# An opening written out as one list of steps, with the first phases rounded by matmul

## The chip, the cores and the metric

The kernel runs on one core of one Trainium2 chip. The core has five engines that run side by side, each through its own instructions in order: TensorE (PE, matmuls; PEld are its weight loads), VectorE (DVE), ScalarE (ACT), GpSimd (POOL) and SyncE (SP). DMA transfers are issued here from SP, POOL and ACT. The metric is the device time of one execution in microseconds (us).

## The reference

The program is a block with two parts. The first convolves a sequence of 2048 tokens with 576 channels by kernels that are sums over 128 complex poles per channel; the second is a gated MLP.

```python
dt = jnp.exp(log_dt)[:, None]
A = A_re + 1j * A_im
logdA = dt * A
P = jnp.exp(logdA[:, :, None] * l[None, None, :])
K = jnp.einsum("dn,dnl,dn->dl", Cc, P, dB).real
...
y = irfft(rfft(u) * rfft(K)) + u * Dskip
...
h = _layernorm(x) * (1 + ca) + sa
x = x + ga * _A_ref(h, ...)
h = _layernorm(x) * (1 + cb) + sb
x = x + gb * _B_ref(h, ...)
```

`sa`, `ca`, `ga`, `sb`, `cb`, `gb` are six rows of `silu(c) @ w_mod`, the modulation rows.

## The kernel before

**Poles.** `poles` turns the inputs (`A_re`, `A_im`, `log_dt` and so on) into four numbers per pole: decay, phase per step, phase per 64 steps, and the weight's logarithm and phase. Each is split in three bf16 parts (`split3`, tiles `pt`) and stored in DRAM (`pa_d` phases, `pb_d` decays), one transfer for each half of the partitions. It runs twice: for chunk 0 on tiles of 128x144, then for chunks 1 to 3 together on 128x432 (`p1`, in steps between other work). `poles_load` fetches a chunk's tables back as `lb`, `lc`, `la`.

**Groups.** 36 groups of 16 channels follow, nine per chunk. For a group g, `e_unit` builds exponents by matmul with a table of small numbers (`sel`) and takes their Exp (tile `et`); `t_unit` builds phases by matmul. For g under 10 they are rounded in PSUM: adding and taking off a large constant (`magics`) by matmul leaves the fraction; DVE copies the result to SBUF (`ft`, L479) and takes its absolute value (L484). For later groups ACT adds the constant (L482) and DVE subtracts (L483). `s_unit` takes the sine of both on ACT, of the absolute value with a quarter turn as its bias, which is the cosine (L489, L490). `p_unit` multiplies exponents with sines and cosines on DVE (L500 to L503), `kg_unit` multiplies the results into the convolution kernel on PE (L513, evacuated as `kab`, L516), `d_unit` adds the skip term, `k1_unit` applies a first transform (L530, L537).

**LN and the input.** Four `x` tiles (`ln_x`) of four rows each are normalized. `ln_stats` takes mean and variance, for the first two tiles on ACT (L397, L400), for the others by DVE's statistics instruction. `ln_pair` scales two rows, multiplies them with small transforms (L433: pieces of 32 rows by 64 columns, four row pieces by two column pieces of the array), evacuates (L435, `st1o`) and stores to `u_d`. It needs three modulation rows (`mod_unit`: 24 matmuls with `ec`, an evacuation `mpart`, two matmuls with `ones`).

**Rounds.** A loop over `tick` (a round) runs one group: exponents for three groups in every third round, phases of group `tick`, sines of `tick - 1`, `p` of `tick - 2`, `kg` and `d` of `tick - 3`, `k1` of `tick - 4`. Rounds 0 to 7 also hold the LN pairs, 3 to 5 the last modulation rows. From round 10 the transformed input is loaded (`u_load`), transformed (`u_unit`), its halves swapped by two POOL transfers, multiplied with the transformed kernel (`z_unit`, round 12 on), transformed back (`v_unit`) and stored. Chunk 1's tables are fetched in round 7, behind the last LN pair, and first used in round 9.

**What sets the order.** A scheduler orders each engine's instructions by their dependencies and the order of the code; instructions issued through a `Pin` keep the program's order. In the opening POOL's table transfers and, up to round 0, DVE and PE are pinned. Pools set how far an engine may run ahead: `ps2` gives two PSUM buffers for phases, wide exponents, LN and modulation alike, `ps1` four for the rest; `ft` has three buffers, `et` five, `ln_x`, `st1o` and `lb` two each. Behind the 40 rounds the MLP follows.

Of the kernel before, what the change touches and what calls it, by code (L numbers as in the profile page):

```python
# [9 lines left out]
F32 = mybir.dt.float32  # L10
# [21 lines left out]
def consts():  # L32
# [64 lines left out]
    sel = np.zeros((112, 2368))  # L97
    sel[:48, :1024] = sel[64:, :1024] = half
# [7 lines left out]
    sel[:48, 1024:1280] = sel[64:, 1280:1536] = rge.reshape(48, 256)  # L106
# [57 lines left out]

def ssm(tc, I, x1_d, consts_s, dram, mod_d, mlp):
# [5 lines left out]
    with ExitStack() as ctx:  # L171
# [7 lines left out]
        pa_d = dram.tile([4, 2, 9, CW // 2], BF, name="pa_d")  # L179
        pb_d = dram.tile([4, 2, 6, CW // 2], BF, name="pb_d")  # L180
# [13 lines left out]
        sel = tb.tile([112, 2368], BF, name="sel", bufs=1)  # L194
# [4 lines left out]
        def poles(c0, c1, Q, own=None):  # L199
# [8 lines left out]
            def split3(*items):  # L208

                n = 3 // (c1 - c0)  # L210
                parts = []
                for i, (src, dst, k) in enumerate(items):
                    if not todo:
                        t_ = ep.tile([128, 3, 432], BF, name="pt")
                        todo.extend(t_[:, :, w * j:w * j + w] for j in range(n))
                    parts.append((src, dst, k, todo.pop(0), t("sq%d" % (i % 2))))
                for src, dst, k, pt, q in parts:
                    A.activation(pt[:, 0], src, AF.Copy)
                    V.tensor_tensor(q, src, pt[:, 0], op=ALU.subtract)
                    A.activation(pt[:, 1], q, AF.Copy)  # L220
                for src, dst, k, pt, q in parts:
# [11 lines left out]
            def run():  # L233
# [3 lines left out]
                A.activation(dt, ldt, AF.Exp)  # L237
                V.tensor_tensor(tau, dt, tau, op=ALU.mult)
# [13 lines left out]
                ax, ay, mx, mn, ph, lw = Cr, Ci, Br, Bi, t("ph"), t("lw")  # L252
# [9 lines left out]
                AP = mlp.tied.scalar  # L262
                AP.activation(q1, mn, AF.Square)
                AP.activation(q1, q1, AF.Ln, bias=one)
                AP.activation(ph, mn, AF.Arctan)
# [4 lines left out]
                split3((al, pb_d, 0), (tau, pa_d, 0))  # L270
# [3 lines left out]
                split3((tau64, pa_d, 3), (lw, pb_d, 3))  # L274
# [15 lines left out]
                split3((ph, pa_d, 6))  # L290
# [5 lines left out]
        def poles_load(c, Q):  # L296
            for n, d_, k in (("lb", pb_d, 0), ("lc", pa_d, 0), ("la", pa_d, 3)):
                t_ = tb.tile([112, 9, 128], BF, name=n)
                if n == "lb":
                    Q.memset(t_[32:64], 0.0)  # L300
                for h in range(2):
                    Q.dma_start(t_[64 * h:64 * h + 48], d_[c, h, k:k + 6].rearrange("q (c g n) -> (q c) g n", c=8, g=9))
                lt[n, c] = t_
# [4 lines left out]
        def halves(t, gi):  # L308
            return [t[64 * h:64 * h + 48, gi] for h in range(2)]

# [15 lines left out]
        def mod_load(k):  # L326
# [6 lines left out]
            for hh in range(2):  # L333
                S.dma_start(wmt[k][hh], I["w_mod"][:, k, hh])
# [7 lines left out]
        def mod_unit(k):  # L342
            wm = wmt.pop(k)
            mpart = ep.tile([128, D], F32, name="mpart", bufs=1)
            pm = ps2()
# [5 lines left out]
            A.activation(v3(mpart), pm[:, :, :HC], AF.Copy)  # L351
# [3 lines left out]
            src = pm[:, :, :HC]  # L355
# [4 lines left out]
            elif k == 0:  # L360
                V.tensor_tensor(v3(sga), src, v3(gar), op=ALU.mult)
                for i in range(2):
                    A.activation(gsp, sga, AF.Copy)
                    V.scalar_tensor_tensor(sga, gsp, msk[:, i:i + 1], sga, op0=ALU.mult, op1=ALU.add)
                A.activation(gsp, sga, AF.Copy)
# [7 lines left out]


        x4s = {}
        r1t = {}

        def ln_load(i):
            x4s[i] = ep.tile([128, 4, D], F32, name="ln_x")
            S.dma_start(x4s[i], I["x"][:, 4 * i:4 * i + 4])  # L380

        def r1_load(i):
            r1t[i] = ep.tile([128, 2, 2, 32], F32, name="r1t"), ep.tile([128, 2, 2, 32], BF, name="cs")
            S.dma_start(r1t[i][0], I["c_r1t"][:, 2 * i:2 * i + 2])
            S.dma_start(r1t[i][1], I["c_cs"][:, 2 * i:2 * i + 2])
# [3 lines left out]
        def ln_stats(i):  # L389
            x = x4s[i]  # L390
            nm = ep.tile([128, 4], F32, name="nm")
            r = ep.tile([128, 4], F32, name="r")
            if i < 2:
                junk = ep.tile([128, 4, HC], F32, name="st1o").rearrange("p (a b) d -> p a (b d)", a=2)
                ss = ep.tile([128, 4], F32, name="ss", bufs=1)
                for b in range(4):
                    A.activation(junk[:, 0], x[:, b], AF.Copy, accum_out=nm[:, b:b + 1])  # L397
                V.tensor_scalar(nm, nm, -1.0 / D, None, op0=ALU.mult)
                for b in range(4):
                    A.activation(junk[:, 1], x[:, b], AF.Square, bias=nm[:, b:b + 1], accum_out=ss[:, b:b + 1])  # L400
                V.tensor_scalar(ss, ss, 1.0 / D, None, op0=ALU.mult)
                rsqrt(V, ep, r, ss, 4)
            else:
                bs = ep.tile([128, 4, 2, 6], F32, name="bs")
                mv = ep.tile([128, 4, 2], F32, name="mv")
                for b in range(4):
                    for h in range(2):
                        V.bn_stats(bs[:, b, h], x[:, b, HC * h:HC * h + HC])
                    V.bn_aggr(mv[:, b], bs[:, b])
                V.tensor_scalar(nm, mv[:, :, 0], -1.0, None, op0=ALU.mult)  # L410
                rsqrt(V, ep, r, mv[:, :, 1], 4)
            lns[i] = nm, r

        def ln_rows(b):
# [5 lines left out]
            V.tensor_scalar(rt, r1t[b // 2][0][:, b % 2].rearrange("p r k -> p (r k)"), r[:, j:j + 1], None, op0=ALU.mult)  # L420
            return n, rt, r1t[b // 2][1][:, b % 2].rearrange("p r k -> p (r k)")

        def ln_pair(b):
            pair = [ln_rows(b), ln_rows(b + 1)]
            for h in range(2):
                c = slice(HC * h, HC * h + HC)
                o = ep.tile([128, 4, HC], F32, name="st1o")
                pms = [ps2(), ps2()]
                for t, (n, rt, cs) in enumerate(pair):
                    for x, y, st in ((cs, gsp, True), (rt, n, False)):  # L430
                        for g in range(4):
                            rows = slice(32 * g, 32 * g + 32)
                            T.matmul(pms[g // 2][64 * t:64 * t + 64, g % 2, :HC], x[rows], y[rows, c], start=st, stop=not st, skip_group_check=True)  # L433
                for k, pm in enumerate(pms):
                    A.activation(o[:, 2 * k:2 * k + 2], pm[:, :, :HC], AF.Copy)  # L435
# [1763 lines left out]
```

## Time and profile before

| what | value |
| --- | --- |
| median of 3 runs | 1783.53 us (1782.89 to 1787.73) |
| span of the profiled execution | 1781.6 us |
| PE, DVE, ACT, POOL busy over the span | 94%, 71%, 47%, 14% |
| bytes moved by DMA | 376.24 MB, 211 GB/s |

The execution's time around its span is not recorded by itself; the median stands 1.9 us above the span. The page draws the span in 40 slices of 44.5 us; each digit is a tenth of the slice that the engine was busy, and PEclk the TensorE clock that was granted, in tenths of full speed:

```profile
PE   3687899997899999999999999999999999999999
DVE  6874999965899998698899778688344478344432
ACT  4766998854477656445434444234232223122210
PEclk9576999998899999999999999999999999999999
DMA  9456645579689879777675886874766573556531
```

The first five digits are the opening: PE and its clock are low there, and neither DVE nor ACT is full. From the fifth slice on (178 us) PE is near full. The views used below have these forms: a table of stages gives the busy time of each engine in a stretch; a group row gives line, engine, operation, output and input tiles, shapes and count, then busy us and mean ns of one, then idle time before them and what ended it; a timeline row gives start and length in us, and in brackets the idle time before it with its releaser. L152 is the line of `Pin`, so pinned instructions are told apart by their tiles.

### The profile page before, as it was taken

Reading aid. Unit: us, or ns where it says so; the run is one execution under the profiler, and the core shown is the slowest. Engines: PE = TensorE matmul, PEld = TensorE weight load, DVE = VectorE, ACT = ScalarE, POOL = GpSimd, SP = SyncE. Lnnn points to the kernel's source line nnn. Section 1 sums busy time; section 2 is a strip of 40 time slices with the busy share of each in tenths; the row PEclk is TensorE's granted clock in tenths of the full one; section 3 lists DMA queues with packets and bytes.
Section 4 is the critical chain, followed back from the end, with each engine's and each line's share of the span. In section 5 each row is a group of like instructions: output and inputs, shape, how many; then the busy total and the mean of one; then the engine's idle time right before and its main releaser. Section 6 shows DMA issues by size and latency. Waiting matters only on the chain.

```text
span 1781.6 us, 36375 instructions
## 1 busy us (share of the span) xinstructions
PE 1671.0 (94%) x15174; PEld 1242.2 (70%) x15174; DVE 1258.9 (71%) x2259; ACT 833.9 (47%) x1118; POOL 244.8 (14%) x400
## 2 busy tenths in 40 slices
PE   3687899997899999999999999999999999999999
PEld 1243555565455545777877888888888888888887
DVE  6874999965899998698899778688344478344432
ACT  4766998854477656445434444234232223122210
POOL 3312232333122211000000000000111100111100
PEclk9576999998899999999999999999999999999999
DMA  9456645579689879777675886874766573556531
GB/s 260 133 179 184 189 124 172 172 204 297 206 260 283 246 229 267 281 245 256 233 224 164 287 302 240 267 244 125 249 219 232 195 234 98 192 195 219 192 111 41
DMA packets 183381, 376.24 MB, mean 211 GB/s; under 512 B 39360, under 2 KB 103488, under 8 KB 182448
## 3 DMA queue, kind: packets, MB, share of 16 engines
q1 hardware_dynamic: 140416, 175.23, 32.7%
q0 software_dynamic: 36896, 172.01, 29.3%
q10 hardware_dynamic: 5904, 26.67, 3.7%
q8 instruction: 119, 1.95, 0.5%
q14 instruction: 46, 0.38, 0.1%
HBM read 263.11 MB, written 101.31 MB: 205 GB/s over the span
## 4 chain that ended last, share of the span: by engine, by line
PE 57%; DVE 16%; DMA 3%; issue 3%; ACT 1%; POOL 0%; ACTq 0%; SPq 0%; DVEq 0%; POOLq 0%
PE ps L152 54%; DVE bsz L152 2%; DVE zset L152 1%; DVE n L152 1%; DVE gt L152 1%; DVE rq L152 1%; DMA zset<-set_d 1%; DVE wsp L152 1%; DMA wsst<-in_w_spT 1%; DVE wso L152 1%; DVE nt L152 1%; DVE raw L152 1%; DVE rx L152 1%; DVE bsx L152 1%; DVE z L152 1%
## 5 line engine op out<-in xcount | busy, mean ns | idle before, releaser
L152 PEld LDWEIGHTS <-zset 128*128 128x128 f16 x7182 | 702.1, 98 | 91.9 <-DVE zset L152 7.6
L152 PE MATMUL ps<-wsp,zset 128*128 128x256 f16 x6048 | 667.4, 273 | 6.9 <-DVE zset L152 5.8
L152 PE MATMUL pz<-wz,nt 128*128 128x512 f16 (+1 forms) x1120 | 223.4, 360 | 8.9 <-DVE nt L152 4.2
L152 ACT ACTIVATE z<-gt 128x1024 f16<-128x1024 f32 x56 | 59.0, 1054 | 288.6 <-DVE gt L152 288.6
L152 PEld LDWEIGHTS <-nt 128*128 128x128 f16 x1120 | 109.9, 99 | 116.3 <-DVE nt L152 5.7
L152 DVE SCALAR_TENSOR_TENSOR gt<-ps,sc,bsp 128x512 f32<-128x512 f32 x36 | 27.0, 749 | 205.0 <-PE ps L152 203.3
L1907 POOL DMA_DIRECT2D zset<-set_d x96 | 50.8, 529 | 868.5 <-PE ps L152 614.6
L152 PE MATMUL ps<-wout,z 128*128 128x288 f16 x1344 | 170.0, 286 | 0.0
L152 PEld LDWEIGHTS <-z 128*128 128x128 f16 x1344 | 131.5, 98 | 33.0
L152 PE MATMUL ps<-n2o,zset 128*128 128x256 f16 x1134 | 128.2, 273 | 0.0
L152 DVE SCALAR_TENSOR_TENSOR gt<-ps,sc,gt 128x512 f32<-128x512 f32 (+1 forms) x180 | 122.2, 696 | 7.9 <-DVE gt L152 0.5
L152 DVE TENSOR_TENSOR raw<-raw 128x512 f32<-128x512 f32 (+2 forms) x228 | 119.1, 528 | 12.3 <-DMA raw<-z_d 7.9
L152 ACT ACTIVATE zset<-raw 128x1792 f16<-128x1792 f32 x48 | 81.0, 1690 | 57.8 <-PE ps L152 23.4
L152 DVE TENSOR_TENSOR zset<-raw,zset 128x1792 f16<-128x1792 f32 x48 | 96.9, 2019 | 14.9 <-ACT zset L152 14.9
L152 DVE TENSOR_TENSOR z<-ps,z 128x512 f32<-128x512 f32 (+1 forms) x126 | 71.9, 598 | 36.8 <-ACT z L152 26.7
L152 ACT ACTIVATE wsp<-raw,sc 128x1792 f16<-128x1792 f32 x25 | 44.6, 1785 | 43.0 <-DVE raw L152 35.3
L152 ACT ACTIVATE z<-z,sc 128x1024 f32<-128x1024 f32 x21 | 24.1, 1149 | 75.6 <-DVE z L152 71.9
L152 ACT ACTIVATE z<-pz,sc 128x512 f32<-128x512 f32 (+1 forms) x96 | 52.3, 579 | 15.0 <-PE pz L152 10.9
L152 PE MATMUL ps<-n2q,wf 128*128 128x512 f16 x252 | 55.7, 379 | 0.0
L152 ACT ACTIVATE z<-z,nm,r 128x1152 f32<-128x1152 f32 x24 | 31.5, 1343 | 50.3 <-DVE nm L152 28.2
L501 DVE TENSOR_TENSOR pg<-et,ft 128x1024 f32<-128x1024 f32 x36 | 43.8, 1217 | 13.3 <-ACT ft L489 11.6
L152 PE MATMUL ps<-wout,z1b 128*128 128x288 f16 x384 | 52.6, 286 | 0.5 <-ACT z1b L152 0.5
(358 smaller groups left out, 2461.9 us busy)
## 6 DMA issues: line engine op xcount, KB each, us to landing
zset<-set_d POOLq DMA_DIRECT2D x96, 896.0 KB, 4.9
raw<-z_d SPq DMA_DIRECT2D x48, 512.0 KB, 5.7
set_d<-zset ACTq DMA_DIRECT2D x24, 896.0 KB, 6.1
z_d<-z POOLq DMA_DIRECT2D x32, 576.0 KB, 9.2
zset<-wa_d POOLq DMA_DIRECT2D x18, 896.0 KB, 4.8
raw<-in_w_spT SPq DMA_DIRECT2D x25, 512.0 KB, 4.4
set_d<-zset SPq DMA_DIRECT2D x12, 896.0 KB, 5.9
u_d<-st1o POOLq DMA_DIRECT2D x16, 576.0 KB, 4.1
```

The costliest lines, as they stand in the source:

```text
L152: return self.tc.keep_in_program_order(f(*a, **k))
L501: V.tensor_tensor(pr, pi, c3[:, :, None, :].to_broadcast([128, 16, 2, 32]), op=ALU.mult)
L1907: self.nc.gpsimd.dma_start(o, self.set_d[f, j - 1] if j else self.wa_d[f])
```

## The change

Six things change.

1. **One list.** `OPENING`, a string, replaces all up to round 13: 396 steps, each a short name with indices and each meant for one engine (`eA`/`EA` exponents by matmul / Exp, `eB`/`EB` the same for the second part, `a`/`A` sine phases / sine, `c`/`C` cosine phases / cosine, `pa`/`pb` the two halves of `p`, `k`/`K` and `n`/`N` the two kernel products and their evacuations, `h`/`H`/`u` LN products, evacuation, store, `w` statistics, `r` row updates, `q` a step of the big pole chain, `mm`, `me`, `mo`, `mf` a modulation row, `X` the fetch of chunk 1's tables, `P` the change of pools). The units are cut into such parts, and all engines are pinned while the list runs. The loop then starts at round 14 with the code of before.
2. **Phases.** For groups under 14 both phases are rounded by matmul. The cosine's quarter turn is a 49th row of the tables, of ones in `lc` and `la` and of ±0.25 in `sel`. The sine reads PSUM; DVE's copy and absolute value go.
3. **LN.** Products come in steps of two row pieces (`ln_mm(j, h, k)`), one PSUM buffer each. The statistics of tile 2 are taken on ACT, of tiles 0, 1 and 3 on DVE. The transform tables of LN (`r1t`, `cs`) come in two transfers instead of sixteen.
4. **Poles.** Both halves of a stored part go in one transfer. Chunk 0's tables are fetched from SP, `lb` ahead of the others, and the big pole inputs are issued behind them.
5. **Loads.** The first `x` tiles, the first modulation row's weights (`mod_load(0)`) and the LN tables are issued from POOL.
6. **Tables of later chunks** are fetched in step `X`, and in rounds 14 and 21 (before: 7, 13 and 21); each fetch has five memsets instead of one.

```diff
+    for c0, q in ((0, 0.25), (768, 0.25), (1536, -0.25)):
+        sel[48::64, c0:c0 + (512 if c0 == 1536 else 256)] = q
...
+OPENING = (
+    "mo 2;mm 1;ml 3;mg 2;me 1;eA 0;w 0 0;mo 1;EA 0;w 0 1;eB 0;w 0 2;w 0 3;eA 1;EB 0;eB 1;EA 1;w 0 4;eA 2;EB 1;eB 2;EA 2;mm 0;EB 2;mf 1;"
+    "q 0;r 0;a 0;me 0;q 1;mo 0;mf 0;q 2;c 0;ga 0;gb 0;q 3;ga 1;gb 1;q 4;r 1;w 1 0;r 2;ga 2;A 0;w 1 1;r 3;w 1 2;h 0 0 0;C 0;w 1 3;"
...
-                        for h in range(2):
-                            Q.dma_start(dst[c, h, k:k + 3].rearrange("q (p f) -> p q f", p=64),
-                                        pt[64 * h:64 * h + 64, :, 144 * (c - c0):144 * (c - c0) + 144])
+                        Q.dma_start(dst[c, k:k + 3].rearrange("q h (p f) -> (h p) q f", p=64),
+                                    pt[:, :, 144 * (c - c0):144 * (c - c0) + 144])
...
+        def poles_tile(c, Q):
+            for n, p in (("lb", 112), ("lc", 113), ("la", 113)):
+                lt[n, c] = tb.tile([p, 9, 128], BF, name=n)
+                Q.memset(lt[n, c][32:64], 0.0 if n == "lb" else 1.0)
+                if n != "lb":
+                    Q.memset(lt[n, c][96:113], 1.0)
...
+        def ln_mm(j, h, k):
+            c = slice(HC * h, HC * h + HC)
+            pm = lno[j, h, k] = ps2()
+            for t in range(2):
+                n, rt, cs = prs[2 * j + t]
+                for x, y, st in ((cs, gsp, True), (rt, n, False)):
+                    for g in (2 * k, 2 * k + 1):
+                        rows = slice(32 * g, 32 * g + 32)
+                        T.matmul(pm[64 * t:64 * t + 64, g % 2, :HC], x[rows], y[rows, c], start=st, stop=not st, skip_group_check=True)
...
+        def phase(g, x):
             c, gi = divmod(g, 9)
+            pa = tp[g, x] = ps2()
+            hv, rw = (halves, rows) if x else (halves1, rows1)
...
-            if g < NR:
-                magics(2112, True)
-                phases((768, 0), False, False)
-                magics(2240, False)
-                phases((1536, 1792), False, True)
-                V.tensor_copy(f, pa)
...
+            magics(2112, True)
+            phases((768, 0), False)
+            magics(2240, False)
+            phases((1536, 1792), True)
+
+        def sine(g, x):
+            if x:
+                tt[g] = tb.tile([128, 2, 2, 512], F32, name="ft", bufs=3)
+            A.activation(tt[g][:, x], tp.pop((g, x)), AF.Sin, scale=-TWO_PI)
...
+        V, A, G, T, S = mlp.tied.vector, mlp.tied.scalar, mlp.tied.gpsimd, mlp.tied.tensor, mlp.tied.sync
...
+        for step in OPENING.split(";"):
+            name, *args = step.split()
+            steps[name](*map(int, args))
+        V, A, G, T, S = nc.vector, nc.scalar, nc.gpsimd, nc.tensor, nc.sync
+        for tick in range(14, NG + 4):
```

How this moves instructions at the places on which the prediction rests, first on ACT. Before, around the first sines (`ft`); `t_q` and `t_ph` belong to the big pole chain, `st1o` are LN evacuations and, with `ss`, LN statistics:

```order
L400 ACTIVATE st1o,ss<-ln_x,nm 128x576
L152 ACTIVATE t_q_307<-t_q_307,consts_s 128x432
L400 ACTIVATE st1o,ss<-ln_x,nm 128x576
L152 ACT_TABLE_LOAD
L152 ACTIVATE t_ph<-t_n_B_im 128x432
L435 ACTIVATE st1o<-ps 128x576 x2
L489 ACT_TABLE_LOAD
L489 ACTIVATE ft<-ft,consts_s 128x1024
```

After the change, from the same chain on:

```order
L154 ACTIVATE t_q_359<-t_q_359,consts_s 128x432
L154 ACTIVATE gsp<-sga 128x576
L154 ACT_TABLE_LOAD
L154 ACTIVATE ft<-ps 128x1024 x2
L154 ACTIVATE st1o<-ps 128x576
L154 ACTIVATE t_ph<-t_n_B_im 128x432
```

Sine and cosine of group 0 now stand ahead of all LN evacuations, and the arctangent (`t_ph`) follows them under the same table. The second place is POOL at the fetch of chunk 1's tables, of before (`u_d` are LN stores, `mod_d` modulation rows):

```order
L372 DMA mod_d<-gar 16x1x36
L436 DMA u_d<-st1o 128x4x288 x6
L152 MEMSET lb 32x1152
L152 DMA lb<-pb_d 48x1152 x2
L152 DMA lc<-pa_d 48x1152 x2
```

and of the change:

```order
L154 DMA u_d<-st1o 128x4x288
L154 MEMSET lb 32x1152
L154 MEMSET lc 32x1152
L154 MEMSET lc 17x1152
L154 MEMSET la 32x1152
L154 MEMSET la 17x1152
L154 DMA lb<-pb_d 48x1x1152 x2
L154 DMA lc<-pa_d 48x1x1152 x2
L154 DMA la<-pa_d 48x1x1152 x2
L154 DMA mod_d<-gar 16x1x36
L154 DMA u_d<-st1o 128x4x288 x2
```

The fetch has moved ahead of eight LN stores and three modulation rows, and four memsets have joined it. A third place, on PE at the start: before, all three modulation rows (weights `wm`, then `k`) stand ahead of the first exponent (`lb`):

```order
L152 MATMUL ps<-wm,ec 32x288 x12
L152 MATMUL ps<-mpart,small 128x288 x2
L152 MATMUL ps<-k_122,ec 32x288 x12
L152 MATMUL ps<-mpart,small 128x288 x2
L152 MATMUL ps<-k_140,ec 32x288 x12
L152 MATMUL ps<-mpart,small 128x288 x2
L152 LDWEIGHTS lb
L152 MATMUL ps<-sel,lb 128x512
```

and in the change:

```order
L154 MATMUL ps<-wm,ec 32x288 x12
L154 MATMUL ps<-mpart,small 128x288 x2
L154 MATMUL ps<-k_122,ec 32x288 x12
L154 LDWEIGHTS lb
L154 MATMUL ps<-sel,lb 128x512
L154 LDWEIGHTS lb
L154 MATMUL ps<-sel,lb 128x512
L154 MATMUL ps<-mpart,small 128x288 x2
```

The third row has moved behind the exponents of the first three groups.

More of the change, by code (lines that the diff above doesn't have):

```diff
@@ L269, in run @@
                 yield
-                split3((al, pb_d, 0), (tau, pa_d, 0))
+                yield from split3((q2, mx), (al, pb_d, 0), (tau, pa_d, 0))
                 yield
@@ L382, in r1_load, with ln_stat @@
[L382 to L385, printed above, removed]
+            Q.dma_start(x4s[i], I["x"][:, 4 * i:4 * i + 4])
         lns = {}
-        def ln_stats(i):
+        lnt = {}
+        def ln_stat(i, b):
             x = x4s[i]
[L391 to L402, printed above, removed]
-            else:
[L404 to L409, printed above, removed]
@@ L456, in ssm, with e_mm @@
-        NR = 10
-        def t_unit(g):
-            c, gi = divmod(g, 9)
-            cs = tb.tile([128, 2, 2, 512], F32, name="ft", bufs=3)
-            ct, f = cs[:, 0], cs[:, 1]
-            pa = ps2()
-            def phases(cols, start, stop):
+        eps = {}
+        def e_mm(g):
+            c, gi = divmod(g, 9)
+            pa = eps[g] = ps2()
+            for h, (l, r) in enumerate(zip(halves(lt["lb", c], gi), rows(256, 512))):
+                T.matmul(pa[:, h], l, r, start=True, stop=True)
@@ L693, in ssm @@
[L693 to L710 removed]
+        poles_load(0, S, ("lc", "la"))
```

366 lines of the change are left out of this document (217 added, 149 removed), and 15 rows, old and new, of the table OPENING.

## The prediction

> **What bounds the kernel now.** The first view is the table of stages: busy time per engine, granted TensorE clock ("PEclk") and DMA share. Columns: stretch in us, its length, then PE, PEld, DVE, ACT and POOL busy (instructions), PEclk, DMA share, GB/s.
>
> ```profile
> 66.00:100.00 34.00, 27.99 (x305) 12.94 (x302) 31.21 (x73) 22.95 (x32) 15.45 (x23) 0.52 0.58 176
> 100.00:160.00 60.00, 48.28 (x777) 26.13 (x773) 36.80 (x75) 39.29 (x58) 11.29 (x16) 0.83 0.55 174
> 160.00:176.00 16.00, 9.27 (x85) 3.91 (x85) 3.56 (x4) 7.48 (x10) 2.45 (x6) 0.51 0.83 224
> 176.00:206.00 30.00, 24.77 (x381) 15.54 (x382) 27.20 (x34) 28.52 (x36) 5.82 (x11) 0.86 0.75 220
> ...
> 66.00:206.00 140.00, 110.31 (x1541) 58.51 (x1541) 98.77 (x185) 98.24 (x134) 35.00 (x54) 0.72 0.63 190
> ...
> 209.20:232.40 23.20, 21.70 (x309) 12.55 (x308) 20.94 (x27) 22.09 (x30) 6.87 (x13) 1.00 0.46 130
> ```
>
> The last row is three rounds of the loop when it runs evenly: ACT is busy 22.09 of 23.20 us (95%), PE 21.70 at full clock, DVE 20.94. The row above it is the part of the opening behind the first sine: ACT and DVE are busy 98 of 140 us, 70%, and no engine is the bound; the engines wait for each other. The page's span says how much room that is in the whole: 40 us of idle ACT is 2.3%.
>
> ```profile
> span 1781.6 us, 36375 instructions
> ```
>
> The second view is the list of waits from 50 to 206 us (engine, line and tile that waited, releaser: us in total, times, longest).
>
> ```profile
> DVE ft L479 <- PE ps L467: 14.8, 3, 11.7
> ACT ft L489 <- DVE ft L484: 14.3, 5, 7.6
> DVE pg L501 <- ACT ft L489: 10.2, 6, 5.8
> PE ps L450 <- DMA lb<-pb_d: 8.1, 2, 6.8
> ```
>
> The phase chain passes from PE over DVE to ACT and back to DVE, and each hand-over is waited for. The last row is one hole of its own. The third view, the timeline, shows it: POOL begins to fetch the pole table of chunk 1 at 157.6 us, behind the last LN store, and PE, which has asked for it since 158.6, starts at 165.4.
>
> ```profile
> 157.63 1.08 POOL L152 MEMSET lb<- 32x1152 bf16 x1
> 159.00 1.31 POOL L152 DMA_DIRECT2D lb<-pb_d  x2 [0.29 <-POOL lb L152]
> ...
> 165.40 0.58 PE L450 MATMUL ps<-sel,lb 48*128 48x512 bf16 x1 [6.76 <-DMA lb<-pb_d]
> ```
>
> **Where the changed opening ends.** Its last step is the first `v`; then comes the loop at round 14, whose instructions are those of before. I take 206 us of before as this point: the first sine of group 14 starts at 209.22, and 3 us of ACT work (sine 13, one `kab`, `uu`, `k` and `v` each) that the loop still has to do lies ahead of it. What is gained at this point I carry to the end undiminished, since all behind it is one chain of rounds and transfers that they trigger.
>
> ```profile
> 65.79 1.15 ACT L489 ACTIVATE ft<-ft,consts_s 128x1024 f32<-128x1024 f32 x1
> ...
> 209.22 1.22 ACT L489 ACTIVATE ft<-ft,consts_s 128x1024 f32<-128x1024 f32 x1
> ```
>
> **The start: when is the first sine?** Before: 65.79. Now it stands on ACT behind the logarithms of the big pole chain (chunks 1 to 3), which wait for DVE. Before:
>
> ```profile
> 21.15 1.35 POOL L152 DMA_DIRECT2D pa_d<-pt  x2 [3.11 <-DMA pb_d<-pt]
> 25.36 1.03 POOL L152 DMA_DIRECT2D lb<-pb_d  x2 [1.76 <-DMA pb_d<-pt]
> ...
> 34.16 0.61 DVE L152 TENSOR_TENSOR t_q<-t_n_C_im,t_n_B_im 128x432 f32<-128x432 f32 x1 [2.66 <-DMA t_n_B_im<-in_A_B_im]
> ...
> 51.16 0.38 DVE L152 TENSOR_SCALAR t_n_C_re<-t_wr 128x432 int32<-128x432 int32 x1
> ...
> 57.63 0.60 DVE L152 TENSOR_TENSOR t_n_B_im<-t_n_B_im,t_rnd 128x432 f32<-128x432 f32 x1
> ```
>
> The last store of the small pole chain leaves at about 20.5 us (21.15 before, 0.6 of it a second half), and must land before SP fetches the tables and, behind them, issues the seven big inputs. With 4 us to land (21.15 to 25.36), 3 to issue and 8 in flight (B_im, issued at 25.25, arrived at 34.1) the inputs are complete near 38, 4 us later than before. DVE then needs 2 us for the products and 5.3 for 51.16 to 57.63 less the 1.2 us copy between, and waits nowhere for the third modulation row as it did before (that wait is what put 17 us between 34.16 and 51.16). With a logarithm, two row shifts and one table load on ACT: first sine at 51, between 47 (inputs no later than before) and 58 (one more transfer of 7 us in the way). Sines 0 are thus 15 us earlier.
>
> **ACT's work behind it.** Start from the 98.24 us busy in 66 to 206. The rows that change (mean ns of one behind the comma):
>
> ```profile
> L435 ACT ACTIVATE st1o<-ps 128x576 f32<-128x576 f32 x32 | 19.4, 645 | 7.4 <-issue 3.3 <-PE ps L433 3.0 <-ACT k L537 0.5
> L489 ACT ACT_TABLE_LOAD x6 | 7.7, 1283 | 0.1
> L400 ACT ACTIVATE st1o<-ln_x,nm 128x576 f32<-128x576 f32 x8 | 6.1, 768 | 0.6 <-DVE nm L152 0.5
> L482 ACT ACTIVATE ft<-ps,consts_s 128x1024 f32<-128x1024 f32 x5 | 5.7, 1140 | 0.8 <-PE ps L467 0.8
> L397 ACT ACTIVATE st1o<-ln_x 128x576 f32<-128x576 f32 x8 | 5.4, 680 | 0.6 <-DMA ln_x<-in_x 0.5
> ```
>
> Groups 10 to 13 lose their rounding pass: 4 x 1.14 = 4.6 off. Table loads behind the first sine fall from 10 to 8: 2.6 off. Statistics of the third LN tile come to ACT: 4 x 0.68 + 4 x 0.77 + eight accumulator reads of 0.19 = 7.3 on. Three LN evacuations that lay ahead of 66: 1.9 on. The sines read PSUM instead of SBUF; the rounding pass that read it took 1.14 like the sine with a bias, so nothing, with ±0.1 each (±2.8 for 28). Sum 100.2 us.
>
> **DVE's work.**
>
> ```profile
> L479 DVE COPY ft<-ps 128x1024 f32<-128x1024 f32 x10 | 12.2, 1217 | 14.8 <-PE ps L467 14.8
> L484 DVE TENSOR_SCALAR ft<-ft 128x1024 int32<-128x1024 int32 x14 | 9.6, 688 | 0.1
> L483 DVE SCALAR_TENSOR_TENSOR ft<-ft,ps 128x1024 f32<-128x1024 f32 x5 | 6.1, 1214 | 1.6 <-ACT ft L482 1.5
> ```
>
> Behind 66 us go 9 copies (11.0), 13 absolute values (8.9) and 4 subtractions (4.9); seven LN row updates of 0.81 come behind the first sine: 98.8 - 24.8 + 5.7 = 80 us. DVE is no longer a bound, and two of the four waits above have nothing left to wait for.
>
> **PE's work.** A phase is 12 matmuls. Below, at full clock, it lasts from 107.32 to the next instruction at 108.29, 0.9 us without the gap; at half clock 1.66 (89.43 to 91.09).
>
> ```profile
> 89.43 0.61 PE L471 MATMUL ps<-sel 48*128 48x512 bf16 x2 [0.26 <-ACT st1o L435]
> ...
> 107.32 0.39 PE L471 MATMUL ps<-sel 48*128 48x512 bf16 x2
> ...
> 108.09 0.27 PE L467 MATMUL ps<-sel,la 48*128 48x256 bf16 x2
> ...
> 114.25 0.34 PE L433 MATMUL ps<-gsp,cs 32*64 32x288 bf16 x6 [0.15 <-ACT gar L369]
> 114.37 0.70 PE L433 MATMUL ps<-ln_x,rt 32*64 32x288 f32 x12
> ```
>
> Cosine and sine each get one, for 14 groups: 26 behind the first pair, 23.4 us at full clock, where 9 whole and 4 short ones stood. An LN half pair took 0.75 us with eight array tiles side by side (114.25 to 115.0); the list halves it into steps of four tiles. Between 12 us (as cheap per matmul as before) and 21 (each half step as long as a whole one but for its overlap, 0.65) for 32 steps I take 21, as the tiles of one step are all that can overlap when something else stands between. Per group the two products behind `p` (`k` and `n` in the list) are 1.03 each and E 0.64 (193.45 to 194.09); three modulation rows took 9.5 with their first products alone (rows of the timeline, of the chain of waits and of the groups):
>
> ```profile
> 193.45 0.39 PE L453 MATMUL pk<-sel,lb 112*128 112x512 bf16 x1
> ...
> 194.09 0.39 PE L453 MATMUL pk<-sel,lb 112*128 112x512 bf16 x1
> ...
> 343.03 1.03 PE pk L513 x64
> ...
> 345.11 1.03 PE pk L530 x16
> ...
> L349 PE MATMUL ps<-wm,ec 96*32 96x288 f32 x72 | 9.5, 574 | 0.0
> ```
>
> That is 11 x 1.03 + 10 x 1.03 + 12 x 0.64 = 29.3; I take 10 for the modulation rows and 8 for the first four `u`, two `z` and one `v` (a `v` as two, each about an `n`). Sum 23.4 + 21 + 29.3 + 18 = 92 us at full clock. Over 140 us before, the mean clock was 0.72; 92 / 0.72 = 128 us would already be more than ACT's 100. **The clock decides who is the bound.** PE is denser now, and in the denser rows of before the clock was 0.83 and 0.86, so I take a mean of 0.85: 108 us.
>
> A rule speaks to this. The row first: from 75 to 80 us PE was busy all the time and the clock stayed at 0.50.
>
> ```profile
> 75.00:80.00 5.00, 5.00 (x38) 1.88 (x34) 5.00 (x11) 1.35 (x2) 5.00 (x9) 0.50 0.81 222
> ```
>
> The Trainium skill, "TensorE: Matmul & The Clock Gate", section "Part 1: The HAM clock gate (the "warmup" mystery)", says that one busy window of about 3.4 us lifts the clock to full. This row does not bear it out for such small matmuls; by the rule PE would cost 92 plus some 2 us, and ACT alone would be the bound: rival (a) below.
>
> **POOL and the pole tables.** Chunk 1's fetch stands eight LN stores earlier in POOL's order, so the hole at 160 us goes. Five memsets at 1.08 now hold POOL for 5.4 us, and the LN stores behind them; two LN buffers cover some of it, and if not, ACT waits about 4 us. In the loop two such fetches meet a POOL that is busy 6.87 of 23.20 us: nothing. The halved number of pole stores saves POOL time that nobody waited for: nothing.
>
> **The sum.** ACT has 100.2 us. At 95% busy (the even rounds) that takes 105.5 us, at 70% (before) 143; the listed order takes out named waits but lets no engine go ahead, so I take the middle, 82.5%: 121.5 us. PE's 108 fit in it at 89%. End of the opening 51 + 121.5 = 172.5 against 206: 33.5 us gained. The span becomes 1748.1; the median of the runs shown, 1783.53, lies 1.9 above the profiled span, so **1750**.
>
> **Rivals.** (a) ACT-bound and tight, as in the even rounds, with PE warm: 51 + 105.5 = 156.5, gain 49.5, 1734. For it: sines need no DVE any more. Against: 92 us of PE work must then run in 105.5. (b) The waits only change names: PE and ACT pass two PSUM buffers to and fro, 70%: 51 + 143 = 194, gain 12, 1772. For it: the third wait above, DVE for a sine, stays, and the same two PSUM buffers carry phases, E, LN and modulation. (c) The change doesn't bring the start forward, since the big inputs now queue behind the tables: first sine at 66, 66 + 121.5 = 187.5, gain 18.5, 1765. (d) Slower: PE stays cold. The extra phases and the split LN steps make PE the only bound, at half clock; with 155 us from 51 to 206 it costs nothing until the mean clock falls below 92 / 155 = 0.59. At the 0.52 of 66 to 100 us it is 92 / 0.52 = 177 us, end at 228, 22 later: 1806. Against it: 0.83 and 0.86 in later rows.
>
> **How the numbers follow.** Forecast 0.55 (1742 to 1760), (a) 0.18, (b) 0.14, (c) 0.06, (d) 0.07. The range reaches from just under (a) to (b): 1731 to 1772. A change under 0.3% (5.4 us) can't be told from none here. Faster: 0.55 + 0.18 + 0.06 + 0.10 of (b) = 0.89; same: 0.04 of (b); slower: 0.07.
>
> **What would show it.** Right: the first sine near 51, ACT busy over 80% from there to the first `v`, the clock mostly full, no PE wait for `lb`. Wrong: first sine after 58; ACT waiting for phases on PE with the clock at 0.5 past 100 us; or the gain shrinking behind round 14.

## The result and the profile after

The changed kernel takes 1799.72 us (median of 4 runs, 1793.07 to 1802.63); the kernel before takes 1783.5. The ratio is 1.0079, 95% interval 1.0056 to 1.0102: **slower** by 0.8%. The forecast was 1750.

The profiled execution of the changed kernel has a span of 1798.0 us, 49.9 above the 1748.1 that the sum gave. The rows below answer to those of before; L154 is now the line of `Pin`, L584 the sine in the loop. First the span, and the first sine and those of groups 14 and 17 in the timeline (start and length in us):

```profile
span 1798.0 us, 36706 instructions
...
83.56 1.02 ACT L154 ACTIVATE ft<-ps 128x1024 f32<-128x1024 f32 x1
...
217.32 1.16 ACT L584 ACTIVATE ft<-ft,consts_s 128x1024 f32<-128x1024 f32 x1 [3.57 <-DVE ft L580]
...
244.20 1.15 ACT L584 ACTIVATE ft<-ft,consts_s 128x1024 f32<-128x1024 f32 x1 [0.24 <-DVE ft L580]
```

The first sine comes at 83.56, not at 51 and not even at the 65.79 of before. The table of stages (stretch, length, busy PE, PEld, DVE, ACT, POOL, then PEclk, DMA share, GB/s) with the stretch behind the first sine and three even rounds:

```profile
66.00:100.00 34.00, 19.41 (x203) 8.96 (x203) 31.93 (x69) 19.60 (x29) 4.49 (x6) 0.60 0.19 63
100.00:160.00 60.00, 52.66 (x814) 29.74 (x807) 47.23 (x109) 47.14 (x77) 23.39 (x32) 0.80 0.66 192
160.00:176.00 16.00, 15.27 (x264) 8.24 (x263) 9.43 (x14) 12.77 (x19) 2.07 (x3) 0.89 0.22 77
...
83.56:214.32 130.76, 117.86 (x1721) 64.42 (x1720) 88.54 (x185) 101.88 (x152) 38.00 (x54) 0.82 0.61 182
244.20:267.40 23.20, 21.88 (x310) 12.72 (x309) 20.74 (x28) 22.04 (x29) 6.01 (x12) 1.00 0.28 85
```

From the first sine to 214.32 (3 us ahead of the sine of group 14, the end as the prediction took it) ACT is busy 101.88 of 130.76 us, 78%, with a mean clock of 0.82. The hole at 160 to 176 us is gone (PE 15.27 of 16 us), and the loop's even rounds are what they were. So most of the loss, 32.6 of the 49.9 us, lies ahead of the first sine. There the stages show this, and the list of waits says for what PE and SP stood still (engine, tile, releaser: us in total, times, longest):

```profile
30.00:40.00 10.00, 0.00 (x0) 0.00 (x0) 5.92 (x26) 0.00 (x0) 0.00 (x0) 0.50 1.01 283
40.00:44.00 4.00, 0.00 (x0) 0.00 (x0) 0.00 (x0) 0.00 (x0) 0.00 (x0) 0.50 0.33 129
44.00:48.00 4.00, 0.00 (x0) 0.00 (x0) 0.00 (x0) 0.00 (x0) 0.00 (x0) 0.50 0.07 28
48.00:52.00 4.00, 0.00 (x0) 0.00 (x0) 0.00 (x0) 0.00 (x0) 0.00 (x0) 0.50 0.10 31
```

```profile
PE ps L154 <- DMA small<-in_c_small: 39.4, 1, 39.4
SPq L154 <- DMA sel<-in_c_sel: 14.1, 1, 14.1
```

Between 40 and 52 us nothing on the core works, and yet something is in flight: the mean share of the 16 DMA engines is 0.07 to 0.10, a little over one engine in sixteen (0.0625). SP's queue shows which transfer. Each row is an issue, with its start and length:

```profile
5.44 0.33 SPq L154 DMA_DIRECT2D sel<-in_c_sel  x1
5.82 12.12 SPq L154 DMA_DIRECT2D k<-in_w_mod  x2
17.98 3.40 SPq L154 DMA_DIRECT2D small<-in_c_small  x1
...
50.08 2.25 SPq L154 DMA_DIRECT2D la<-pa_d  x2
53.58 0.42 SPq L154 DMA_DIRECT2D t_n_log_dt<-in_A_log_dt  x1
```

SP waits for `sel` for 14.1 us before it issues `la` and, behind it, the seven big pole inputs at 53.58; PE waits 39.4 us for `small`, which stands behind `sel`. The quarter turn made `sel` a table of 113 rows in place of 112. The trace keeps each row of it as one packet of 4736 bytes:

```
kernel            packets  first start to last end  most in flight at once
before            112       2.97 us                 19
changed           113      38.84 us                  2
```

112 rows went out side by side, 113 go nearly one after another, never more than two at once. This was not in the prediction in any form.

### The profile page after: what moved, and what is told of

Read it like the earlier page. It is cut to its first block, busy times and chain, and to the rows that moved or that the text cites. A ratio compares the mean times of both kernels' runs of the same rounds, so it can differ in the third digit from the quotient of the medians.

```text
span 1798.0 us, 36706 instructions
## 1 busy us (share of the span) xinstructions
PE 1673.5 (93%) x15374; PEld 1247.2 (69%) x15374; DVE 1244.5 (69%) x2242; ACT 819.0 (46%) x1095; POOL 252.6 (14%) x397
## 4 chain that ended last, share of the span: by engine, by line
PE 42%; DVE 18%; issue 9%; DMA 7%; ACT 3%; POOL 1%; ACTq 0%; SPq 0%; DVEq 0%; POOLq 0%
PE ps L154 40%; DMA zset<-set_d 4%; DVE zset L154 4%; DVE gt L154 2%; DVE bsz L154 2%; DMA raw<-z_d 1%; ACT z L154 1%; DVE n L154 1%; DVE rq L154 1%; DVE wsp L154 1%; DVE raw L154 1%; DVE wout L154 1%; DVE wso L154 1%; DVE z L154 1%; DMA uu<-v_d 1%
## 5 line engine op out<-in xcount | busy, mean ns | idle before, releaser
L154 PEld LDWEIGHTS <-zset 128*128 128x128 f16 x7182 | 702.7, 98 | 95.5 <-DVE zset L154 7.5
L154 PE MATMUL ps<-wsp,zset 128*128 128x256 f16 x6048 | 669.4, 273 | 9.0 <-DVE zset L154 5.8
L154 PE MATMUL pz<-wz,nt 128*128 128x512 f16 (+1 forms) x1120 | 222.3, 358 | 11.2 <-DVE nt L154 4.3
L154 ACT ACTIVATE z<-gt 128x1024 f16<-128x1024 f32 x56 | 59.0, 1054 | 292.6 <-DVE gt L154 292.6
L154 PEld LDWEIGHTS <-nt 128*128 128x128 f16 x1120 | 108.9, 98 | 118.3 <-DVE nt L154 5.8
L154 DVE SCALAR_TENSOR_TENSOR gt<-ps,sc,bsp 128x512 f32<-128x512 f32 x36 | 27.0, 750 | 207.2 <-PE ps L154 205.5
L154 PE MATMUL ps<-wout,z 128*128 128x288 f16 x1344 | 170.0, 286 | 0.0
L154 PEld LDWEIGHTS <-z 128*128 128x128 f16 x1344 | 131.5, 98 | 33.0
L154 DVE TENSOR_TENSOR raw<-raw 128x512 f32<-128x512 f32 (+2 forms) x228 | 119.2, 528 | 14.7 <-DMA raw<-z_d 10.4
L154 PE MATMUL ps<-n2o,zset 128*128 128x256 f16 x1134 | 128.2, 273 | 0.0
L154 DVE SCALAR_TENSOR_TENSOR gt<-ps,sc,gt 128x512 f32<-128x512 f32 (+1 forms) x180 | 122.2, 696 | 7.6
L154 ACT ACTIVATE zset<-raw 128x1792 f16<-128x1792 f32 x48 | 81.0, 1690 | 55.3 <-PE ps L154 18.7
L154 DVE TENSOR_TENSOR zset<-raw,zset 128x1792 f16<-128x1792 f32 x48 | 96.9, 2019 | 13.1 <-ACT zset L154 13.1
L154 DVE TENSOR_TENSOR z<-ps,z 128x512 f32<-128x512 f32 (+1 forms) x126 | 72.0, 599 | 37.2 <-ACT z L154 26.7
L154 ACT ACTIVATE wsp<-raw,sc 128x1792 f16<-128x1792 f32 x25 | 44.6, 1785 | 43.1 <-DVE raw L154 35.4
L154 ACT ACTIVATE z<-z,sc 128x1024 f32<-128x1024 f32 x21 | 24.1, 1148 | 76.0 <-DVE z L154 72.3
L154 ACT ACTIVATE z<-pz,sc 128x512 f32<-128x512 f32 (+1 forms) x96 | 51.6, 583 | 12.7 <-PE pz L154 6.1
L154 ACT ACTIVATE z<-z,nm,r 128x1152 f32<-128x1152 f32 x24 | 31.5, 1342 | 56.7 <-DVE nm L154 31.4
L154 PE MATMUL ps<-n2q,wf 128*128 128x512 f16 x252 | 55.7, 379 | 0.0
L154 PE MATMUL ps<-wout,z1b 128*128 128x288 f16 x384 | 52.4, 286 | 0.0
L154 DVE SCALAR_TENSOR_TENSOR wsp<-raw,sc,wsp 128x1792 f16<-128x1792 f32 x25 | 52.0, 2078 | 0.0
```

The lines of the kernel that those rows point to most:

```text
L154: return self.tc.keep_in_program_order(f(*a, **k))
```

## The experiments

**1. `sel` in two transfers, and 113 rows in the kernel of before.** The first kernel is the changed one with

```diff
-        S.dma_start(sel, I["c_sel"])
+        S.dma_start(sel[:112], I["c_sel"][:112])
+        S.dma_start(sel[112:], I["c_sel"][112:])
```

> The changed kernel, with the table of small numbers (sel, 113 rows of 4736 bytes) loaded by two transfers, of 112 rows and of one row, in place of one of 113. Theory T (113 rows go through one DMA engine: in the changed kernel their packets follow each other from about 12 to 50 us, and SP waits 14.1 us for them): the rows land within some 12 us of their issue, as 112 rows did before; the pole inputs are issued near 35 us in place of 53.6, the first sine comes at 60 to 66 us in place of 83.6, and the time is 1776 to 1783 us if all 18 us are carried to the end. Rival R1 (the start is late because the tables and pole inputs stand behind other transfers in SP's and POOL's order): first sine still after 78 us, time above 1793. Rival R2 (the start counts for nothing, the opening is bound by what follows on PE): first sine near 63 but the first sine of group 14 still after 210, time above 1793.

The second is the kernel of before with one more row in the table, which nothing reads:

```diff
-    sel = np.zeros((112, 2368))
+    sel = np.zeros((113, 2368))
...
-        sel = tb.tile([112, 2368], BF, name="sel", bufs=1)
+        sel = tb.tile([113, 2368], BF, name="sel", bufs=1)
```

> The kernel of before with nothing but a row of zeros added to sel: one transfer of 113 rows in place of 112, the new row read by nothing. T: the packets of sel go one after another for 30 to 40 us, small and the pole inputs behind it are late, the first sine comes at 75 to 90 us in place of 65.8, and the kernel is 8 to 25 us slower (1792 to 1808). R1 and R2: no change, 1780 to 1788 us, first sine within 2 us of 65.8.

The split kernel took 1775.57 us, ratio to before 0.9945 (0.9924 to 0.9965); its packets went out in 2.65 us, up to 20 at once. Before with 113 rows took 1804.36, ratio 1.0111 (1.0093 to 1.0130); 28.37 us, two at once. The first sines in the timeline, of the split kernel and then of before with 113 rows:

```profile
62.63 1.02 ACT L154 ACTIVATE ft<-ps 128x1024 f32<-128x1024 f32 x1
```

```profile
83.59 1.15 ACT L489 ACTIVATE ft<-ft,consts_s 128x1024 f32<-128x1024 f32 x1
```

T holds from both sides: the one row puts 20.9 us on the changed kernel's start, and 17.8 on that of before (65.79 to 83.59); the medians differ by 24.2 and 20.2. R1 and R2 fall. Without the row's transfer the change is a gain, of 0.55%, a quarter of what was forecast. The rest of the runs looks for the other three quarters.

**2. The start: order or bytes?** From here on the kernels are made from the split one unless said otherwise. In the first the big pole inputs are issued right behind `small`:

```diff
+        p1 = poles(1, 4, G)
         poles_tile(0, G)
...
-        p1 = poles(1, 4, G)
```

> As e1_sel_split, and the seven big pole inputs are issued right behind small, ahead of chunk 0's tables, as in the kernel of before. In e1_sel_split they landed from 44 us on, DVE waited 5.1 us for them, and first sine came at 62.6. Theory S (what is left of the late start is the order of SP's queue): the chain starts behind the first exponentials near 40 us, first sine at 55 to 59, and all of it is carried to the end: 4 to 7 us under e1_sel_split, 1769 to 1772. Rival D (DMA is full to 50 us, so moving one transfer ahead makes another late): first exponential later by as much (39 or later in place of 35.7), first sine within 2 us of 62.6, time within 3 us of 1775.6.

1782.47 us, ratio 0.9998 (0.9984 to 1.0012). The timeline of ACT has the first exponential and the first sine:

```profile
42.14 1.02 ACT L154 ACTIVATE et<-ps 128x1024 f32<-128x1024 f32 x1 [14.70 <-PE ps L154]
...
67.23 1.94 ACT L154 ACTIVATE ft<-ps 128x1024 f32<-128x1024 f32 x2
```

D holds, and by more than it expected: the tables now wait behind the inputs, the exponentials come 6.5 us later (35.66 in the split kernel) and the sine 4.6. (The profiled execution took 1777.06 us and is the fastest of eleven.) Next, bytes are taken out of the way, the second `x` tile going last:

```diff
-        ln_load(1, G)
         S.dma_start(dsk, I["dsk"])
+        ln_load(1, S)
```

> As e1_sel_split, but the second x tile (ln_x, 1.18 MB) is fetched by SP behind the pole inputs and dsk, in place of POOL at 26 us. Theory D (bytes: the 16 DMA engines are full to 50 us, so what lies ahead of the pole inputs delays them by its bytes, 4 to 5 us): the pole inputs land by 41, first sine at 57 to 60 us, time 2 to 5 us under e1_sel_split (1771 to 1774). Rival: the start hangs on SP's issues and not on bytes: first sine within 1.5 us of 62.6, time within 2 us of 1775.6.

First sine 60.63, 2 us earlier, and 1776.32 us, ratio 0.9949 (0.9929 to 0.9968): the sine gained half of what D expected, and the end shows no gain.

**3. Sines ahead of the logarithms.** In the list `A 0;C 0;a 1;c 1` move ahead of `ga 0` and `A 1;C 1` behind `q 3`; once on top of the kernel with the inputs first, once on top of that with `ln_x` late.

> As e3_inputs_first, and in the list phases and sines of groups 0 and 1 stand ahead of the logarithms of the big pole chain. Theory L (the order of ACT in the list makes PE wait 12.8 us for the first sine while ACT idles): first sine at 46 to 50 us, 4 sines (4.1 us) less one more table load (1.3) come off ACT's later work: 2 to 5 us under e3_inputs_first. Rival: the LN products need the chain's end anyway, and ACT waits there instead: within 1.5 us of e3_inputs_first.

> As e7_lnx_late, with phases and sines of groups 0 and 1 ahead of the logarithms of the big pole chain, as in e4_sines_first. If ACT's idle time there is worth filling (e4_sines_first was about 5 us under e3_inputs_first): first sine near 47 us, 2 to 5 us under e7_lnx_late. Rival: the time that DVE's chain needs sets the next step in both, and the end moves by less than 1.5 us.

1777.35 (0.9975, 0.9956 to 0.9994), 5.1 under the kernel it builds on, and 1772.57 (0.9932, 0.9909 to 0.9955), 3.7 under its own, which the intervals don't part. In the first kernel the first sine is at 54.05, 4 us behind the 46 to 50 expected; in the second it is at 44.02, 7 us earlier than I had forecast for the whole change, and still the first `v` comes at 191.01, where the kernel it builds on has 192.19. One stage of the second kernel and of the one it builds on tells why, first with the sines ahead, then without:

```profile
100.00:120.00 20.00, 20.00 (x200) 9.10 (x198) 13.06 (x31) 10.74 (x19) 4.80 (x7) 0.50 0.55 151
```

```profile
100.00:120.00 20.00, 18.50 (x327) 10.72 (x321) 18.26 (x42) 18.54 (x32) 8.69 (x11) 1.00 0.80 233
```

With the clock at 0.50, PE is busy all 20 us and gets through 200 matmuls; at 1.00 it gets through 327 in 18.5. It is not the mix alone: the same matmul, `ps<-sel` with 512 columns, takes 622 ns on the mean in the first row and 379 in the second. In this execution the early start was given back here: PE was the bound at half clock. But it took 1781.45 us and is the slowest of six, 8.9 us over their median, so it can't tell what the faster ones did at this place.

**4. The memsets in the loop.** Those of `lc` and `la` for chunks 2 and 3 go:

```diff
-                Q.memset(lt[n, c][32:64], 0.0 if n == "lb" else 1.0)
-                if n != "lb":
+                if n == "lb" or c < 2:
+                    Q.memset(lt[n, c][32:64], 0.0 if n == "lb" else 1.0)
+                if n != "lb" and c < 2:
                     Q.memset(lt[n, c][96:113], 1.0)
```

> As e1_sel_split, without the memsets of lc and la for chunks 2 and 3, whose 49th rows nothing reads. Theory M (the four memsets of 1.05 us in rounds 14 and 21 hold POOL's swaps of the transformed input at the entry of the loop, where DVE waits for them): 2 to 4 us under e1_sel_split. Rival N (prediction: POOL has room there): within 1.5 us of 1775.6.

1775.61 us, ratio 0.9950 (0.9932 to 0.9968): no gain seen, as predicted, though intervals as wide as this and the split kernel's don't exclude the 2 us of M. The traces say more: from the sine of group 14 to that of 17, where the first of the two fetches lies, this kernel takes 26.88 us (202.38 to 229.26), and so do the changed kernel and the one with the inputs first (198.88 to 225.76), which have the memsets; the split kernel takes 28.13.

**5. The list without the cosine on TensorE, and the reverse.** In the list, each group gets one phase; DVE copies it out and takes the absolute value, ACT adds the quarter turn:

```diff
-            A.activation(tt[g][:, x], tp.pop((g, x)), AF.Sin, scale=-TWO_PI)
+            t = tt[g][:, x]
+            A.activation(t, t, AF.Sin, scale=-TWO_PI, **({} if x else {"bias": halfpi}))
+
+        def frac(g):
+            phase(g, 1)
...
+            V.tensor_copy(f, tp.pop((g, 1)))
+            V.tensor_single_scalar(ct.bitcast(I32), f.bitcast(I32), 0x7FFFFFFF, op=ALU.bitwise_and)
```

> As e1_sel_split, but with one phase per group below 14, copied from PSUM by DVE with the absolute value taken there, and the cosine with a quarter turn as ACT's bias: the phases of before in the listed order. 14 phases of 12 matmuls less on PE (13 us at full clock), 14 copies of 1.22 and 14 absolute values of 0.69 (26.7 us) more on DVE, whose busy time between first sine and first v goes from 88.6 to 115 us of 128. Theory P (the cosine on TensorE is what takes the hand-overs out): DVE becomes late, 4 to 12 us over e1_sel_split (1779 to 1788). Rival Q (PE, busy 113 of 128 us there, is what the opening waits for, and the list alone does the work): 3 to 10 us under it (1766 to 1773).

1797.29 us, ratio 1.0077 (1.0061 to 1.0093): P, and about twice its price, 21.7 us over the split kernel. (The list was written for two phases and is not put in a new order for one, so this prices this list without the cosine, not every list.) The waits between 60 and 220 us show the old hand-overs back in place:

```profile
ACT ft L154 <- DVE ft L154: 25.7, 10, 4.5
DVE ft L154 <- PE ps L154: 18.8, 9, 4.6
```

The reverse is made from the kernel of before, with its scheduler and its LN; both sines stand right behind their phases, a round earlier than before, and the 49th rows are set for chunks 0 and 1 alone:

```diff
+                for x in (1, 0):
+                    if not x:
+                        hv, rw = halves1, rows1
+                    pa = ps2()
...
+                    A.activation(cs[:, x], pa, AF.Sin, scale=-TWO_PI)
```

> The kernel of before with part 2 of the change alone (and sel loaded by two transfers): for groups under 14 sine and cosine phases by matmul with the 49th row, both sines from PSUM, right behind their phases; no list, order by the scheduler. Theory P1 (the cosine on TensorE gains by itself, the list is not needed for it): 5 to 15 us faster than before, 1769 to 1779. Rival P2 (without the list the two PSUM buffers that phases share with exponents and LN stand full, and ACT's order is another): within 4 us of before, or slower.

1797.49 us, ratio 1.0068 (1.0049 to 1.0088): P2. One cause stood in its waits, the hole of before grown by the four memsets:

```profile
PE pk L468 <- DMA lb<-pb_d: 10.7, 1, 10.7
```

**6. What the hole is worth.** The kernel of before with one number changed, and the cosine kernel with the same:

```diff
-            if tick in (7, 13, 21):
+            if tick in (6, 13, 21):
```

> The kernel of before with chunk 1's pole tables fetched in round 6 in place of round 7, nothing else. If the hole at 160 us (PE waits 6.8 us for lb) is worth its length, as the prediction had it: 5 to 7 us faster than before, 1776 to 1779. Rival: the LN stores and sums that stood ahead come later by as much, or PE waits for the next thing (the transformed input u): within 2.5 us of before.

> As e8_cosine_only (part 2 of the change without the list), with chunk 1's pole tables fetched in round 6 in place of round 7. In e8_cosine_only the five memsets stood behind the last LN store and PE waited 10.7 us for lb at 165 us. Theory H (the hole alone made e8_cosine_only slow, the cosine on TensorE is worth as much without the list as in it): 1765 to 1774, at or under e10_fetch_early (1773.6). Rival W (the cosine on TensorE gains only against what the list takes away): 1780 to 1788, 10 to 14 us over e10_fetch_early's side of the same fetch, that is 9 to 17 us under e8_cosine_only.

Before with the early fetch: 1773.60 us, ratio 0.9937 (0.9920 to 0.9954), twice the 5 to 7 us expected and as much as the split kernel with all of its six parts. The cosine kernel with it: 1785.98, ratio 1.0014 (1.0002 to 1.0026), 11.5 under its median without, so W; PE still waits 2.0 us for `lb` there. One round earlier still:

> As e10_fetch_early, with chunk 1's tables fetched in round 5. If the fetch in round 6 was still on the path: 1769 to 1772; if it was off it already, within 2 us of 1773.6, or later by the LN stores that now stand behind the fetch.

1772.03, ratio 0.9933 (0.9919 to 0.9948). That is on the border of both expectations, and the times don't decide; the trace of round 6 does, in which PE waits for no table of chunk 1 any more, so there the fetch was off PE's path already. This kernel, the one with the early sines (1772.57) and the one of round 6 (1773.60) have the lowest medians of the study, and their intervals tell them apart neither from each other nor from the split kernel's.

## Why the prediction was wrong

**By its own terms.** In the profiled execution the 49.9 us between 1748.1 and 1798.0 lie as follows; the first two rows are the terms of the sum.

| step | predicted | measured | late by |
| --- | --- | --- | --- |
| first sine | 51 | 83.56 | 32.6 |
| from it to the end of the opening | 121.5 | 130.8 | 9.3 |
| sine of group 14 to that of 17 | 21.7, as before (209.22 to 230.94) | 26.9 | 5.2 |
| behind that | as before | 3.1 longer | 3.1 |

(They add to 50.2; 0.2 of the 0.3 over is that I took 206.22 as 206.) From group 17 to the last sine the changed kernel stays 13.25 us behind; the last row, 3.1, is no more than what executions of this kernel differ by. The split kernel, whose span of 1774.5 us is still 26.4 over the sum, has 11.6 in the first row, 6.8 in the second, 6.4 in the third and 1.7 in the last (0.2 over again): its first sine of group 14 is at 193.97, that of group 17 at 222.10.

**The step that failed** is "the inputs are complete near 38", with "3 to issue and 8 in flight", and behind it "first sine at 51". Two things were wrong in it. The larger is one that it never looked at: part 2 of the change was costed by its matmuls, and the transfer that brings its 113th row was costed by nothing. 20.9 of the 32.6 us went when that row had its own transfer. None of the rivals held it: (c), a start that doesn't come forward, put the first sine at 66, for another reason. The share of the DMA engines and the packets show that the 113 rows ran on about one engine. Why 113 rows do so and 112 don't, the Trainium skill says, "DMA: Bandwidth & Descriptors", section "Why a DMA increments its semaphore by 16 and not by 1": a transfer uses the largest number of engines up to 16 that divides the sizes of the slowest dimension on both sides; 112 is 7 times 16, 113 is prime. The traces agree: 38.8 and 28.4 us with 113 rows, 2.6 to 3.0 with 112.

The smaller part, 11.6 us, is left with the transfer split. "3 to issue" was mis-sized: SP issued the first input at 28.27 and the last at 43.27 (15.0 us), and single issues took up to 5.77 us where others took 0.4. The first rows are from the split kernel; the second show that the kernel of before had it already, with 16.9 us from the first input's issue to the last one's:

```profile
28.27 0.44 SPq L154 DMA_DIRECT2D t_n_log_dt<-in_A_log_dt  x1
...
31.93 5.77 SPq L154 DMA_DIRECT2D t_n_A_re<-in_A_A_re  x1
...
43.27 0.53 SPq L154 DMA_DIRECT2D t_n_B_im<-in_A_B_im  x1
```

```profile
8.34 0.43 SPq L231 DMA_DIRECT2D t_n_log_dt<-in_A_log_dt  x1
...
15.98 6.01 SPq L231 DMA_DIRECT2D t_n_C_re<-in_A_C_re  x1
...
25.25 0.69 SPq L231 DMA_DIRECT2D t_n_B_im<-in_A_B_im  x1
```

On DVE the chain waits for the second input, and its products, which the prediction starts at 38, start at 49.73 in the split kernel:

```profile
44.83 0.61 DVE L154 TENSOR_TENSOR t_n_A_im<-t_dt,t_n_A_im 128x432 f32<-128x432 f32 x1 [5.10 <-DMA t_n_A_im<-in_A_A_im]
...
49.73 0.60 DVE L154 TENSOR_TENSOR t_wr<-t_n_C_re,t_n_B_re 128x432 f32<-128x432 f32 x1
```

Of these 11.7 us, 6.8 go until that input has landed, 16.0 us after its issue and not 8, and 4.9 with the steps of DVE in between, which the sum left out (1.2 of it a wait for a modulation row). From the products to the first sine it is 12.9 us for 13 predicted. Moving the inputs ahead made the tables late instead (1782.47 us), so the two shared something that was full: the DMA share of the split kernel is 1.02 from 28 to 36 us.

**The stretch behind the first sine** was close in its parts. ACT had 101.88 us to do for 100.2 predicted, at 78% for 82.5%, and the clock was 0.82 for 0.85. Of the 9.3 us, 2.0 are ACT's added work and the rest is the lower share. The other engines were sized low: PE was busy 117.86 us for 108, DVE 88.54 for 80. What was wrong is what the gain in it was put down to. The views from the first sine to the end of the first `v`, for before, before with the early fetch, the cosine alone with early fetch, the list alone, and the split kernel, in this order (one execution each; that of the third kernel is the fastest of eleven, 1781.57 us):

```profile
65.79:202.43 136.64, 107.00 (x1480) 56.38 (x1476) 95.39 (x182) 94.88 (x129) 32.22 (x49) 0.72 0.63 191
```

```profile
64.11:189.77 125.66, 102.37 (x1480) 54.82 (x1476) 95.29 (x182) 94.20 (x129) 32.15 (x49) 0.78 0.67 207
```

```profile
56.26:196.80 140.54, 118.43 (x1620) 66.10 (x1621) 78.71 (x170) 102.06 (x143) 36.52 (x54) 0.77 0.61 185
```

```profile
64.60:213.08 148.48, 115.24 (x1552) 63.31 (x1545) 111.38 (x209) 101.83 (x153) 37.98 (x53) 0.70 0.53 162
```

```profile
62.63:189.95 127.32, 112.73 (x1721) 62.49 (x1720) 88.45 (x184) 101.86 (x152) 37.79 (x53) 0.87 0.62 185
```

The 136.64 us of before shrink to 125.66 by the early fetch alone, at the same work, and to 127.32 by the whole change with the transfer split. Of the 11.0 us of the early fetch, 6.3 are idle time of PE and 4.6 its busy time for the same 1480 matmuls, at a clock of 0.78 for 0.72; whether the moved fetch raised the clock isn't shown. At the 95% of the even rounds ACT's 94.88 us of before would take 100, so of some 37 us that I read as hand-overs 11 went with one hole, which the prediction named and didn't price.

With the early fetch, which the list has too, the medians are 1773.60 us with neither list nor cosine, 1785.98 with the cosine, 1797.29 with the list and 1775.57 with both ("list" stands for parts 1, 3, 4 and 5 together). So list and cosine brought nothing on net beyond the fetch, each alone loses, and they need each other: the cosine takes DVE out of the way (88.45 us busy for 111.38 in the list alone), and takes PE in (112.73 of 127.32). No run has both with the fetch left in its old place. That the scheduler's order suffers from the cosine because PE becomes its bound (118.43 of 140.54 us at a clock of 0.77) is read from that row and not tried; the other place of the sines on ACT is a rival that no run parts from it.

Right were: PE no longer waits for `lb` at chunk 1, and the memsets in the loop cost nothing that the runs show. Rival (d) did not decide, but half of it is seen in experiment 3: a stage with PE full at half clock.

**The entry of the loop.** From the sine of group 14 to that of 17 the changed kernel takes 5.2 us more, which the prediction had at nothing: it took both kernels to stand at the same place 3 us ahead of the sine of group 14. The two stretches, before and after the change:

```profile
209.22:230.94 21.72, 20.22 (x302) 11.50 (x301) 19.71 (x25) 20.61 (x29) 5.85 (x11) 1.00 0.44 125
```

```profile
217.32:244.20 26.88, 25.64 (x393) 15.19 (x393) 22.65 (x28) 22.79 (x31) 14.66 (x21) 1.00 0.77 213
```

PE is nearly full in both, and runs 393 matmuls for 302: 256 of `kg` for 192, 64 of `k1` for 48, one group's worth more. That group is missing ahead of the sine of group 14, where 704 of `kg` are done for 768; behind group 17 it is 1344 in both. So the 5.2 us are work of PE, 5.4 us, which the kernel of before has done earlier. Up to an equal point the changed kernel is thus late by some 14.5 us behind its first sine, and not by 9.3.

## What to carry to other kernels

Look at the shape of every transfer that a change touches, small constants included: a row more can put a load on one DMA engine, and its sign in the profile is a DMA share near 0.06 while SP and PE wait. Before a rewrite, price each single hole by itself: here one moved fetch gave as much as the six parts together, with the row's transfer split. Two parts that each lose may gain together, so test parts alone and in pairs before the gain is put down to one.

## What the runs showed of the hardware

A transfer of 113 rows of 4736 bytes took 38.8 and 28.4 us where 112 rows took 3.0. It held up a transfer behind it on the same queue too: in the kernel of before `small`, 384 KB, landed 17.5 us after its issue, with the added row 25.1, and in the changed kernel 36.4.

The clock did not follow PE's load in this opening. In experiment 3 it was granted at 0.50 through 20 us in which PE was busy for all 20.00, against 1.00 in a stage of the kernel next to it with 18.50 of 20. The rule weighed in the prediction (the Trainium skill, "TensorE: Matmul & The Clock Gate", section "Part 1: The HAM clock gate (the "warmup" mystery)": one busy window of about 3.4 us lifts the clock) is not borne out by that stage. The mean over the stretch differs between kernels from 0.70 to 0.87, and with it what PE's work costs; a forecast for an opening like this has to carry that as a range.
